# Five transposes ahead of a late weight chunk, and the next tile's transposes one matmul later

## Chip, cores, metric

One core of a Trainium2 chip. The metric is the device time of one execution in microseconds. The kernel before took 253.84 us (median of three runs, 253.70 to 254.02).

In the profile lines PE is the matmul engine and PEld its row of weight loads; DVE is VectorE, ACT ScalarE, and SP the engine that issues the loads from memory. A line gives start (us), duration (us), engine, line of the kernel, operation, written <- read, shapes and count; in square brackets stands how long the engine was idle just before, and what the profile says ended it.

## The reference, cut to what matters

```python
xn = layernorm(x)                        # x: 2048 tokens x 640, bf16
q, k, v = split(xn @ wqkv)               # 640 -> 3 * 640
out = x + local_attention(q, k, v) @ wo + ((xn @ w_gate) * (xn @ w_up)) @ w_down
```

The change concerns the first 18 us only: the layer norm of the first four tiles of 128 tokens, their transposes, and the first Q and K products.

## The kernel before

A recording layer takes operations in program order, finds their dependences and writes one instruction stream for each engine, in that order. The order in which the Python calls stand is the order on PE.

Loads, all issued by SP one after the other. The Q weights come in five chunks (c, 128 input channels each), then K's:

```python
x_load(1)
for c in range(NCH): wqkv_load(0, c)     # Q weights, chunks 0..4
x_load(2); x_load(3)
for c in range(NCH): wqkv_load(1, c)     # K weights
for t in range(4, 8): x_load(t)
x_load2(8); wqkv_load(2)                 # ... V weights in one piece
```

A tile is normalised by DVE into XNS, transposed by PE in five pieces into PSUM and copied to XNT. For tile 1 DVE copies pieces 0 and 1, ScalarE pieces 2 to 4 (some lines cut):

```python
def tr(t, c0=0):
    ln_pe(t, c0)        # transposes c0..4 of tile t on PE
    ln_copy(t)          # the copies PSUM -> XNT
    if t == 1: ...      # layer norm of tiles 2 and 3 on DVE

def proj_tile(which, t, b, bm, at={}):   # Q (which = 0) of one tile, 25 matmuls of 128 columns
    for c, m in [(c, m) for c in range(NCH) for m in range(NCH)]:
        if (c, m) in at: at[c, m]()
        ... matmul of weights chunk c, column block m, with XNT[:, c, tile t]

bm = 1
proj_tile(0, 0, 0, bm, {(4, 0): lambda: ln_pe(1, 0, 2), (4, 3): lambda: tr(1, 2)})
part_evac(0, 0, 1, 0, 4, 0, 0)
proj_tile(0, 1, 2, bm)
...
for c in range(NCH):                     # K of tiles 0 and 1, 25 matmuls of 256 columns
    if c in (2, 3): tr(c)
    for m in range(NCH): ...
```

After this come Q and K of tiles 2 and 3 (50 matmuls of 256 columns), then V (512 columns) and everything else, without a pause in the matmul stream.

Of the kernel before, what the change touches and what calls it, by code (L numbers as in the profile page):

```python
# [215 lines left out]
def build_kernel(nc, A_x, A_wqkv, A_wo, B_x, B_w_gate, B_w_up, B_w_down, out):  # L216
# [145 lines left out]
    def tp_view(t, c0, c1):  # L362
        b = tp_banks[t % 2]
        if t == 0:
            b = (6, 3, 3, 4, 4)[c0]
        if t == 1 and c0 > 1:
            b = 4
        if t == 2 and c0 > 2:
            b = 5
        return PS[:, b, :].bitcast(BF16)[:, c0 * 128:c1 * 128].rearrange("p (c f) -> p c f", c=c1 - c0)  # L370

    def ln_stats_a(t):
        if t >= NT:
            return
        x, st = XST[:, t % NXS, :], STATS[:, t % 2, 0:12]
        op("dve", lambda e: e.bn_stats(st[:, 0:6], x[:, 0:DHALF]), r=[x[:, 0:DHALF]], w=[st], name=f"bna{t}")

    def ln_stats_b(t):
        if t >= NT:
            return  # L380
        x, st = XST[:, t % NXS, :], STATS[:, t % 2, 0:12]
        op("dve", lambda e: e.bn_stats(st[:, 6:12], x[:, DHALF:D]), r=[x[:, DHALF:D]], w=[("stb", t)], name=f"bnb{t}")

    def ln_aggr(t):
        if t >= NT:
            return
        st, mv, sd = STATS[:, t % 2, 0:12], MV[:, t, 0:2], SD[:, t, 0:1]
        op("dve", lambda e: e.bn_aggr(mv, st), r=[st, ("stb", t)], w=[mv], name=f"bnag{t}")
        op("act", lambda e: e.activation(sd, mv[:, 1:2], ACT.Sqrt, bias=EPSC[:, 0:1]), r=[mv, EPSC[:]], w=[("sd", t)],
           name=f"sd{t}")  # L390
# [13 lines left out]
    def ln_rstd(t):  # L404
        if t >= NT:
            return
        sd, rstd = SD[:, t, 0:1], SD[:, t, 1:2]
        op("dve", lambda e: e.reciprocal(rstd, sd), r=[("sd", t)], w=[("rstd", t)], name=f"rstd{t}")

    def ln_apply(t, between=None):  # L410
        if t >= NT:
            return
        x, xs, mv = XST[:, t % NXS, :], XNS[:, t % NXN, :], MV[:, t, 0:2]
        sd, rstd = SD[:, t, 0:1], SD[:, t, 1:2]
        op0 = ALU.add if t == 1 else ALU.subtract
        mean = ("nm", t) if t == 1 else mv
        if between is None:
            ln_rstd(t)
        else:
            between()  # L420
        for c0, c1 in {0: ((0, 128), (128, D)), 1: ((0, 256), (256, D))}.get(t, ((0, D),)):
            o, i = xs[:, c0:c1], x[:, c0:c1]
            op("dve", (lambda o, i: lambda e: e.tensor_scalar(o, i, mv[:, 0:1], rstd, op0=op0, op1=ALU.mult))(o, i),
               r=[i, mean, ("rstd", t)], w=[o], name=f"lnap{t}")
        if t >= NTP:
            o = XNT[:, :, t * TS:(t + 1) * TS]
            op("sp", lambda e: e.dma_start_transpose(o, xs), r=[xs], w=[o], dma=True, name=f"xT{t}")
        if t == 7:
            x_load(13)
            x_load2(14)  # L430
        if t == NT - 1:
            late_loads()

    def ln_pe(t, c0=0, c1=NCH):
        for c in range(c0, c1):
            o = tp_view(t, c, c + 1)[:, 0, :]
            i = XNS[:, t % NXN, c * 128:(c + 1) * 128]
            op("pe", (lambda o, i: lambda e: e.transpose(o, i, IDENT[:]))(o, i), r=[i, IDENT[:]], w=[o], name=f"tr{t}_{c}")  # L438

    def ln_copy(t, only=(0, 1, 2)):  # L440
        parts = ((("dve", 0, 1), ("dve", 1, 3), ("dve", 3, NCH)), (("dve", 0, 2), ("act", 2, NCH)),
                 (("dve", 0, 3), ("act", 3, NCH)), (("act", 0, NCH),))[t]
        for k, (eng, c0, c1) in enumerate(parts):
            if k not in only:
                continue
            o = XNT[:, c0:c1, t * TS:(t + 1) * TS]
            tpv = tp_view(t, c0, c1)
            if eng == "dve":
                op("dve", (lambda o, i: lambda e: e.tensor_copy(o, i))(o, tpv), r=[tpv], w=[o], name=f"xntcp{t}_{c0}")
            else:  # L450
                op("act", (lambda o, i: lambda e: e.activation(o, i, ACT.Copy))(o, tpv), r=[tpv], w=[o],
                   name=f"xntcp{t}_{c0}")
# [15 lines left out]
    def wcols(which, c, m):  # L468
        return WQKV[:, which, c, m:D:NCH]
# [19 lines left out]
    def proj_tile(which, t, b, bm, at={}):  # L489
        for c, m in [(c, m) for c in range(NCH) for m in range(NCH)]:  # L490
            if (c, m) in at:
                at[c, m]()
            o = PS[:, b, m * TS:(m + 1) * TS] if m < 4 else PS[:, bm, t * TS:(t + 1) * TS]
            l, x = wcols(which, c, m), XNT[:, c, t * TS:(t + 1) * TS]
            st, sp = c == 0 and m in (0, 4), c == NCH - 1 and m in (3, 4)
            op("pe", (lambda o, l, x, st, sp: lambda e: e.matmul(o, l, x, start=st, stop=sp))(o, l, x, st, sp),  # L496
               r=[l, x], w=[o], name=f"pp{which}_{m}_{t}_{c}")
# [8 lines left out]
    def part_evac(which, t0, nt, m0, nm, b, col):  # L506
        p = 0 if which == 0 else PAD
        o = (QH, KH)[which][0][:, m0:m0 + nm, p + t0 * TS:p + (t0 + nt) * TS]
        i = PS[:, b, col:col + nm * nt * TS].rearrange("p (m s) -> p m s", m=nm)
        sc = SCALE if which == 0 else 1.0  # L510
        op("act", lambda e: e.activation(o, i, ACT.Copy, scale=sc), r=[PS[:, b, :]], w=[o], name=f"ppev{which}_{m0}_{t0}")
# [224 lines left out]
    def ln_start(t):  # L736
        ln_stats_a(t)
        ln_stats_b(t)
        ln_aggr(t)

    def tr(t, c0=0):
        ln_pe(t, c0)
        ln_copy(t)
        if t == 1:
            ln_start(2)
            ln_stats_a(3)
            ln_stats_b(3)
            ln_rstd(2)
            ln_apply(2, lambda: ln_aggr(3))
# [12 lines left out]
            t_ln[0] += 1.45  # L762

    bm = 1
    proj_tile(0, 0, 0, bm, {(4, 0): lambda: ln_pe(1, 0, 2), (4, 3): lambda: tr(1, 2)})
    part_evac(0, 0, 1, 0, 4, 0, 0)
    proj_tile(0, 1, 2, bm)
    part_evac(0, 1, 1, 0, 4, 2, 0)
    ln_apply(3)
    for c in range(NCH):  # L770
        if c in (2, 3):
            tr(c)
        for m in range(NCH):
            o = PS[:, bm, 2 * TS:] if m == 4 else PS[:, 3 + m // 2, m % 2 * 2 * TS:(m % 2 + 1) * 2 * TS]
            l, x = wcols(1, c, m), XNT[:, c, 0:2 * TS]
            st, sp = c == 0 and m % 2 == 0, c == NCH - 1 and m in (1, 3, 4)
            op("pe", (lambda o, l, x, st, sp: lambda e: e.matmul(o, l, x, start=st, stop=sp))(o, l, x, st, sp),  # L777
               r=[l, x], w=[o], name=f"pw1_{m}_0_{c}")
# [9 lines left out]
    for g in range(5):  # L788
# [6 lines left out]
        else:  # L795
            which, m = ((0, 0), (0, 2), None, (1, 0), (1, 2))[g]
# [161 lines left out]
def bass_parallel_sum__sliding_local_dilated__glu_gated_bilinear__prompt_kernel(  # L958
    nc, A_x, A_wqkv, A_wo, B_x, B_w_gate, B_w_up, B_w_down, out
):  # L960
    build_kernel(nc, A_x, A_wqkv, A_wo, B_x, B_w_gate, B_w_up, B_w_down, out)
# [28 lines left out]
```

## Time and profile before

| | kernel before |
|---|---|
| time, median of 3 | 253.84 us |
| span of the profiled execution | 251.6 us |
| PE busy | 248.1 us (99%) |
| first load of K's weights into the array | 9.26 us |
| first matmul of Q, K for tiles 2 and 3 | 12.60 us |
| first of the last five matmuls | 248.89 us |

PE is the bound. Weight loads run ahead of their matmuls (9.26 against 9.31 us for K's first), so the start of a load shows best when PE was let go. I therefore follow one landmark through all runs, the first load of K's weights. The profile lines themselves stand in the prediction.

### The profile page before, as it was taken

The page shows a single profiled execution, that of the slowest core. Times are in us where ns is not written, and L with a number is a line of the kernel's source. Part 1 is how long each engine was busy: PE and PEld are TensorE (multiplying, and loading weights), DVE is VectorE, ACT ScalarE, POOL GpSimd, SP SyncE. Part 2 cuts the span into 40 slices and gives each one's busy share as a digit, 9 for nine tenths or more (in the row PEclk, how much of TensorE's full clock was granted, in tenths as well). Part 3 has the DMA queues.
Part 4 walks back from the last instruction along what each step waited for, and adds up shares of the span by engine and source line. Part 5 has one row for each costly group of instructions (what it writes and reads, how often), then busy time and mean ns, then how long its engine had stood idle before and what let it go on. Part 6 is the DMA issues. An engine that isn't in the chain of part 4 may idle for free.

```text
span 251.6 us, 3277 instructions
## 1 busy us (share of the span) xinstructions
PE 248.1 (99%) x1294; PEld 128.7 (51%) x1294; DVE 215.7 (86%) x255; ACT 114.6 (46%) x203; POOL 32.5 (13%) x41
## 2 busy tenths in 40 slices
PE   8999999999999999999999999999999999999996
PEld 3995555555544444444444444444444444445775
DVE  4898799999999953999999994999999999995221
ACT  5486657555555557555555553225555011111000
POOL 1000001044434231002331110002000000200200
DMA  6999779774777462355369942297500011581651
GB/s 187 311 261 209 110 200 411 170 122 86 129 146 135 76 125 42 140 197 104 63 126 268 453 151 42 42 337 57 89 0 3 21 42 21 76 114 23 95 136 52
DMA packets 33775, 33.78 MB, mean 134 GB/s; under 512 B 17984, under 2 KB 30272, under 8 KB 33728
## 3 DMA queue, kind: packets, MB, share of 16 engines
q1 hardware_dynamic: 27280, 24.13, 33.8%
q0 software_dynamic: 6192, 9.31, 22.8%
q8 instruction: 10, 0.16, 0.3%
q10 hardware_dynamic: 288, 0.13, 0.2%
q14 instruction: 5, 0.04, 0.1%
HBM read 14.42 MB, written 4.59 MB: 76 GB/s over the span
## 4 chain that ended last, share of the span: by engine, by line
PE 96%; DMA 1%; SPq 1%; issue 0%; DVE 0%
PE PS L642 41%; PE PS L669 22%; PE PS L479 21%; PE PS L701 7%; PE PS L503 2%; DMA WQKV<-in_A_wqkv_dram 1%; PE PS L777 1%; SPq L298 1%; PE PS L496 1%; PE PS L438 0%; DVE FOUT L705 0%
## 5 line engine op out<-in xcount | busy, mean ns | idle before, releaser
L642 PE MATMUL PS<-XNT,WU 128*128 128x512 bf16 x240 | 59.6, 379 | 0.0
L642 PE MATMUL PS<-XNT,WG 128*128 128x512 bf16 x240 | 59.6, 379 | 0.0
L479 PE MATMUL PS<-XNT,WQKV 128*128 128x512 bf16 x250 | 54.1, 379 | 0.0
L609 DVE TENSOR_TENSOR PVB<-VO,ATB 128x10240 f16<-128x10240 bf16 x8 | 43.9, 5490 | 0.2
L479 PEld LDWEIGHTS PS<-XNT,WQKV 128*128 128x128 bf16 x250 | 29.4, 118 | 24.4
L644 ACT ACTIVATE USX<-PS 128x512 bf16<-128x512 f32 x48 | 28.7, 597 | 22.6 <-PE PS L642 22.2
L642 PEld LDWEIGHTS PS<-XNT,WU 128*128 128x128 bf16 x240 | 23.5, 98 | 28.3
L642 PEld LDWEIGHTS PS<-XNT,WG 128*128 128x128 bf16 x240 | 23.5, 98 | 28.3
L604 DVE TENSOR_TENSOR PVB<-PVB 128x5120 f16<-128x5120 f16 (+1 forms) x16 | 34.5, 2156 | 0.3
L537 POOL DMA_DIRECT2D LOG<-PE x24 | 21.9, 924 | 58.4 <-DMA LOG<-PE 58.4
L644 ACT ACTIVATE HT<-PS 128x512 bf16<-128x512 f32 x36 | 21.5, 597 | 16.4 <-PE PS L642 16.4
L675 ACT ACTIVATE DT<-PS 128x512 f16<-128x512 f32 x15 | 8.9, 596 | 42.7 <-PE PS L669 42.7
L669 PE MATMUL PS<-HT,WD 128*128 128x512 bf16 x120 | 27.5, 379 | 0.0
L526 DVE TENSOR_TENSOR TMP<-QH,KH 128x2048 f16<-128x2048 bf16 x16 | 19.2, 1219 | 0.0
L669 PEld LDWEIGHTS PS<-HT,WD 128*128 128x128 bf16 x120 | 11.7, 98 | 14.2
L526 DVE TENSOR_TENSOR PP<-QH,KH 128x2048 f16<-128x2048 bf16 x16 | 18.9, 1219 | 0.0
L669 PE MATMUL PS<-VO,WO 128*128 128x512 bf16 x75 | 18.6, 379 | 0.0
L531 DVE TENSOR_TENSOR PP<-PP,TMP 128x4096 f16<-128x4096 f16 x8 | 18.3, 2291 | 0.2
L705 DVE TENSOR_TENSOR FOUT<-PS,XR 128x320 bf16<-128x320 f32 (+2 forms) x9 | 4.1, 455 | 15.4 <-PE PS L701 15.4
L537 POOL DMA_DIRECT2D PE<-PP x8 | 8.3, 1043 | 63.0 <-DVE PP L532 63.0
L647 DVE TENSOR_TENSOR HT<-HT,USX 128x512 bf16<-128x512 bf16 x36 | 14.4, 418 | 1.7 <-ACT USX L644 1.7
L486 ACT ACTIVATE VO<-PS 128x512 bf16<-128x512 f32 x20 | 11.9, 596 | 8.5 <-PE PS L479 8.4
(71 smaller groups left out, 221.4 us busy)
## 6 DMA issues: line engine op xcount, KB each, us to landing
PE<-PP POOLq DMA_DIRECT2D x8, 512.0 KB, 4.8
ATB<-LOG SPq DMA_DIRECT2D x8, 512.0 KB, 4.9
LOG<-PE POOLq DMA_DIRECT2D x24, 128.0 KB, 2.7
WG<-in_B_w_gate_dram SPq DMA_DIRECT2D x1, 1920.0 KB, 7.9
WU<-in_B_w_up_dram SPq DMA_DIRECT2D x1, 1920.0 KB, 14.6
WD<-in_B_w_down_dram SPq DMA_DIRECT2D x1, 1920.0 KB, 10.1
out_dram<-in_A_x_dram SPq DMA_DIRECT2D x1, 1920.0 KB, 10.3
out_dram<-FACC POOLq DMA_DIRECT2D x3, 640.0 KB, 6.7
```

What stands on the lines that cost most here:

```text
L479: op("pe", (lambda l, x, c: lambda e: e.matmul(PS[:, b, :], l, x, start=(c == 0), stop=(c == NCH - 1)))(l, x, c), r=[l, x], w=[PS[:, b, :] ...
L486: op("act", lambda e: e.activation(o, PS[:, b, :], ACT.Copy, scale=sc), r=[PS[:, b, :]], w=[o], name=f"pev{which}_{m}_{j}")
L526: return (1.22, lambda: op("dve", lambda e: e.tensor_tensor(o, qw, kw, ALU.mult), r=[q, k], w=[o], name=f"prod{h}_{p}_{c}"))
L531: (2.3, lambda: op("dve", lambda e: e.tensor_tensor(a, a, b, ALU.add), r=[a, b], w=[a], name=f"psum{h}_{p}")),
L537: op("pool", lambda e: e.dma_start(o, i, accum_op=ALU.add), r=[o, i], w=[o], dma=True, name=name)
L604: return lambda: op("dve", lambda e: e.tensor_tensor(o, x, y, ALU.add), r=[x, y], w=[o], name=f"{name}_{b}")
L609: lambda: op("dve", lambda e: e.tensor_tensor(PVB[:], vw, aw, ALU.mult), r=[v, a], w=[PVB[:]], name=f"pv_{b}")),
L642: op("pe", (lambda l, x, c: lambda e: e.matmul(PS[:, b, :], l, x, start=(c == 0), stop=(c == NCH - 1)))(l, x, c), r=[l, x], w=[PS[:, b, :] ...
L644: op("act", lambda e: e.activation(o, PS[:, b, :], ACT.Copy), r=[PS[:, b, :]], w=[o], name=f"guev{which}_{m}_{j}")
L647: h_pending.append(lambda: op("dve", lambda e: e.tensor_tensor(h, h, o, ALU.mult), r=[h, o], w=[h], name=f"h{m}_{j}"))
L669: op("pe", (lambda l, x, i: lambda e: e.matmul(PS[:, b, :], l, x, start=(i == 0), stop=(i == n - 1)))(l, x, i), r=[l, x], w=[PS[:, b, :]], ...
L701: op("pe", (lambda l, x, i, b, wid: lambda e: e.matmul(PS[:, b, 0:wid], l, x, start=(i == 0), stop=(i == n - 1)))(l, x, i, b, wid), r=[l, ...
```

## The change

The intent is to use the time in which PE waits for the last chunk of the Q weights. All of tile 1's transposes, two of which stood ahead of that chunk and three behind its third matmul, now stand ahead of it. As PE should then reach tile 2's transposes sooner, these go behind one more matmul.

```diff
-    proj_tile(0, 0, 0, bm, {(4, 0): lambda: ln_pe(1, 0, 2), (4, 3): lambda: tr(1, 2)})
+    proj_tile(0, 0, 0, bm, {(4, 0): lambda: tr(1)})
...
     for c in range(NCH):
-        if c in (2, 3):
-            tr(c)
         for m in range(NCH):
+            if (c, m) in ((2, 1), (3, 0)):
+                tr(c)
```

Only PE's order changes; DVE, ScalarE, GpSimd and SP have the same instructions in the same order.

## The prediction

> **What bounds the kernel now.** I read the page first, then the chain of waits, then the stretch from 5 to 19 us instruction by instruction, because the change touches nothing else. The page says who is full:
>
> ```profile
> PE 248.1 (99%) x1294; PEld 128.7 (51%) x1294; DVE 215.7 (86%) x255; ACT 114.6 (46%) x203; POOL 32.5 (13%) x41
> ```
>
> A matmul engine that is busy 99% of the span can gain only in its few holes or by dropping instructions, and the change drops none. The chain that ended last shows where the unbroken matmul stream begins:
>
> ```profile
> 3.55 3.73 DMA WQKV<-in_A_wqkv_dram
> 7.28 0.05 issue
> 7.33 0.36 PE PS L496 x3
> ...
> 249.34 0.02 issue
> ```
>
> The fifth chunk (c = 4) of the Q weights is issued at 3.55 and lands at 7.28 us; from the matmul it releases at 7.33 the chain is PE alone until the last evacuation. The list of waits gives PE one more hole only, 1.0 us at the very start. So a microsecond saved just behind 7.33 us is a microsecond off the end, unless a later input is not ready. The timeline of that stretch (start, duration, engine, line, operation):
>
> ```profile
> 6.73 0.37 DVE L423 TENSOR_SCALAR XNS<-XST,MV,SD 128x384 bf16<-128x384 bf16 x1
> 6.87 0.28 PE L438 MATMUL PS<-IDENT,XNS 128*128 128x128 bf16 x2
> 7.32 0.21 PEld L496 LDWEIGHTS PS<-XNT,WQKV 128*128 128x128 bf16 x3 [0.34 <-DMA WQKV<-in_A_wqkv_dram]
> 7.33 0.36 PE L496 MATMUL PS<-XNT,WQKV 128*128 128x128 bf16 x3 [0.17 <-DMA WQKV<-in_A_wqkv_dram]
> 7.53 0.33 PE L438 MATMUL PS<-IDENT,XNS 128*128 128x128 bf16 x3
> 7.70 1.78 PE L496 MATMUL PS<-XNT,WQKV 128*128 128x128 bf16 x27
> 7.89 0.49 ACT L451 ACTIVATE XNT<-PS 128x384 bf16<-128x384 bf16 x1 [1.66 <-PE PS L438]
> 9.31 1.26 PE L777 MATMUL PS<-XNT,WQKV 128*128 128x256 bf16 x10
> 9.78 0.39 DVE L423 TENSOR_SCALAR XNS<-XST,MV,SD 128x640 bf16<-128x640 bf16 x1
> 10.29 0.37 PEld L438 LDWEIGHTS PS<-IDENT,XNS 128*128 128x128 bf16 x5
> 10.40 0.44 PE L438 MATMUL PS<-IDENT,XNS 128*128 128x128 bf16 x5
> 10.43 0.45 DVE L423 TENSOR_SCALAR XNS<-XST,MV,SD 128x640 bf16<-128x640 bf16 x1
> ```
>
> Two things are to be seen. First, the weight-load row stands still for 0.34 us before 7.32: two transposes of tile 1 are done, the third to fifth are queued behind matmuls that need the late chunk, although their input is complete at 6.73 + 0.37 = 7.10. Second, there is a hole that the waits do not name. From 7.70 to 9.31 are 27 matmuls in 1.61 us, which is 60 ns each, while the 128-column matmuls near the end of the kernel start every 56 ns (12 from 248.22 to 248.89). 27 x 0.0558 = 1.506, so 0.10 us is missing. Narrow windows find it in the weight loads:
>
> ```profile
> 8.26 0.12 PEld L496 LDWEIGHTS PS<-XNT,WQKV 128*128 128x128 bf16 x1
> ```
>
> ```profile
> 8.44 0.12 PEld L496 LDWEIGHTS PS<-XNT,WQKV 128*128 128x128 bf16 x1
> ```
>
> The load due at 8.26 + 0.056 = 8.32 comes at 8.44. It is the first of chunk 2 of tile 1's Q product (two matmuls end tile 0, ten are chunks 0 and 1), which needs the ScalarE copy of transposes 2 to 4. That copy ran from 7.89 to 8.38 and started when the fifth transpose was done. So the late transposes cost PE twice.
>
> **What the Trainium skill says.** "TensorE: Matmul & The Clock Gate", section "Wait — 56ns, not 53.3ns?": warm matmuls start N / 2.4 GHz + about 2.5 ns apart, 55.6 ns at N = 128. The trace agrees (0.67 us / 12 = 56 ns), and at 256 columns too (50 matmuls from 12.60 to 18.06, 109 ns each). Its section "Part 4: PE-mode transpose" says that a transpose is a matmul into PSUM that needs a copy after it, and gives about 275 ns for one in a kernel's context. Here one is recorded at 220 ns, and in a row they take (7.70 - 7.53) / 3 = 57 ns of the stream; this is what I use. "Perfetto Trace Analysis", section "Tensor Engine Instruction (MATMUL, LD_WEIGHTS)": the recorded end of a matmul is estimated, not observed. Hence I take gaps from starts; the 0.17 us of idle PE that the profile prints beside 0.34 us on the load row is an instance. "DMA: Bandwidth & Descriptors", section "Anatomy of one DMA — SWDGE (gpsimd) path": the DMA engines themselves wait on no semaphore, the issuing sequencer does. SP's order is the same in both kernels, and its weight issues before 10 us stand back to back (0.43 us each), so the landings should stay where they are.
>
> **The change part by part.** Compared engine by engine, only PE's order differs; all counts are equal.
>
> (a) Transposes 2 to 4 of tile 1 move ahead of chunk 4. Earliest start: input ready 7.10, plus the 0.055 us that I see from a DVE end to a PE start (tile 0: 5.11 to 5.16), gives 7.155; loads at 7.155, 7.21 and 7.27, so the fourth slot is 7.32. The chunk's first load was at 7.32. They fit into the hole with nothing left over. Saving: 3 x 0.057 = 0.17 us. Their PSUM target, bank 4, was last read by tile 0's copies, over by 5.97.
>
> (b) The fifth transpose ends about 0.3 us sooner (7.53 + 0.33 = 7.86 before; now start 7.33 + 0.22 = 7.55), so the ScalarE copy runs from about 7.58 to 8.07. Chunk 2 of tile 1 now comes at about 7.33 + 0.03 (restart) + 15 x 0.056 = 8.20. The hidden stall goes: 0.10 us. Chunks 0 and 1 come at 7.64 and need the DVE copy that ended at 7.48 before.
>
> Sum offered to the K product: 0.17 + 0.10 = 0.27 us.
>
> (c) What can take it back. The first K chunk was needed by a load at 9.26. The issue queue and the landing view:
>
> ```profile
> 4.97 2.33 SPq L298 DMA_DIRECT2D WQKV<-in_A_wqkv_dram  x5
> ```
>
> ```profile
> WQKV<-in_A_wqkv_dram SPq DMA_DIRECT2D x1, 160.0 KB, 4.0
> ```
>
> So K chunk 0 lands at 4.97 + 4.0 = 8.97 (the 4.0 is rounded, 8.92 to 9.02), and with the 0.04 us from landing to load seen at 7.28 and 7.32 the load can start at 9.01. Room: 0.25 us. Chunk 1: load 9.80, ready 5.44 + 4.0 + 0.04 = 9.48, room 0.32. Chunk 2 now meets its first matmul where the transposes of tile 2 stood, 10.29: issued 5.91, 4.1 to landing, ready 10.05, room 0.24.
>
> (d) Tile 2's transposes one matmul later. XNS of tile 2 is ready at 9.78 + 0.39 + 0.055 = 10.225, fixed by DVE, which waited for x of tile 2 at 7.74 and for nothing on PE since. Shifted by 0.25 the transposes would come in the load row at 10.04 and wait 0.18. The matmul put ahead takes 0.11 of that, and since loads run 0.11 us ahead of their matmuls (10.29 against 10.40), the rest costs PE at most a few hundredths. Tile 3's transposes: ready 10.43 + 0.45 + 0.055 = 10.935, matmul at 11.23 - 0.25 = 10.98: just in time. Tile 3's ScalarE copy moves with them, its engine free from about 11.43.
>
> (e) Behind that: V's weights land at 9.71 + 7.8 = 17.51, needed by a load at 17.95 (room 0.40); token tiles 4 to 7 land by 18.74 + 4.2 = 22.94, needed near 23.4 (room about 0.4). The attention output for the first down projection is done at 149.95 and used at 152.31. No cap below 0.27.
>
> The smallest room is 0.24 to 0.25, and a stall restarts with a loss of some 0.03. I put the gain at 0.22 us: 253.84 - 0.22 = 253.62 us, or 0.09%.
>
> **The rivals.** *The wait only moves.* If K chunk 0 lands at 9.02 or later in most runs, or tile 2's input is the true gate, 0.05 to 0.15 us comes back: 253.70 to 253.80. For it: the room in (c) and (d) equals the gain almost exactly, and the transfer queue has no slack. Against: four separate gates all leave about 0.24, and the author's matmul ahead of tile 2's transposes opens the tightest. *Transposes get in the way.* If tile 1's second normalisation ends later than 7.10 in other runs, or the wait on it costs more, the three transposes delay chunk 4 by 0.05 to 0.15 us and gain little: 253.75 to 253.95. For it: they fit with nothing left over. Against: even if late, they only go back to where they were, and (b) stays. *The gain is hidden later*, by DVE or a transfer: 253.84. Against: PE waits nowhere after 7.33, with 2.36 us of room at the first down projection. A gain above 0.3 us has no source.
>
> **Range and chances.** The three runs before spread over 0.32 us (253.70 to 254.02), more than the whole effect, so the range is mostly that noise around 253.62: 253.30 to 253.95. Two per cent is 5.1 us, twenty times what the holes hold: within 2% 0.985; faster 0.005; slower 0.01, for an unforeseen state of the chip.
>
> **What would show it.** Right: five transposes in a row from about 6.87, the fifth starting near 7.33; the load of chunk 4 still near 7.32; the ScalarE copy of tile 1 near 7.58 instead of 7.89; 30 matmuls without a hole; the first 256-wide matmul near 9.05 instead of 9.31; the first 512-wide one near 17.84 instead of 18.06. Wrong: chunk 4's load after 7.40 with a wait on DVE; a wait for the weights at K's chunk 0 or 2, or for XNS before tile 2's transposes, longer than 0.1 us; or a first 512-wide matmul 0.2 us earlier with an unchanged end, which would mean that something past 18 us holds the end.

## The result

| | before | after |
|---|---|---|
| median of 6 runs | 253.58 us | 253.34 us |
| all runs | 253.22 to 254.02 | 253.17 to 253.74 |
| span of the profile | 251.6 us | 251.6 us |
| first of the last five matmuls | 248.89 us | 248.82 us |

The ratio is 0.9992 with a 95% interval of 0.9979 to 1.0005. Ratios here are not quite the ratio of the medians. The time lies inside the range and in the class that was predicted, and the ratio of 0.9992 is 0.2 us, near the 0.22 us forecast; but the interval contains 1, which is no effect, and the profile shows only 0.07 us at the end (248.89 - 248.82). The hit on the time is luck in part. The median of the kernel before over all six runs, 253.58, lies in the predicted range as well, so no effect at all would have met it; and the forecast point, 253.62, was worked out from the first three runs (253.84), which were the slower ones. The timeline of the changed kernel at the same place:

```profile
6.76 0.32 PEld L496 LDWEIGHTS PS<-XNT,WQKV 128*128 128x128 bf16 x5 [0.32 <-DVE SD L408]
6.79 0.45 PE L496 MATMUL PS<-XNT,WQKV 128*128 128x128 bf16 x5 [0.20 <-DMA WQKV<-in_A_wqkv_dram]
7.02 0.32 PEld L438 LDWEIGHTS PS<-IDENT,XNS 128*128 128x128 bf16 x5
7.30 1.87 PEld L496 LDWEIGHTS PS<-XNT,WQKV 128*128 128x128 bf16 x30
7.38 0.29 DVE L449 COPY XNT<-PS 128x256 bf16<-128x256 bf16 x1 [0.27 <-PE PS L438]
7.55 0.49 ACT L451 ACTIVATE XNT<-PS 128x384 bf16<-128x384 bf16 x1 [1.30 <-PE PS L438]
9.21 1.14 PEld L777 LDWEIGHTS PS<-XNT,WQKV 128*128 128x128 bf16 x11
```

Several steps look as forecast. The five transposes stand in a row, the load of chunk 4 comes at 7.30 (forecast 7.32), and the ScalarE copy starts at 7.55 (forecast 7.58). Yet the 30 loads last from 7.30 to 9.17. At 0.056 us each the last would end at 7.30 + 29 x 0.0557 + 0.12 = 9.04, so the matmuls are not "without a hole". The first transpose came at 7.02 instead of 6.87, because chunk 3 of the Q weights, on time in the profile before, was late: PE waited for it ahead of 6.79. And K's first load at 9.21 is later than the stream offers: the last load before it begins at 9.05, so 9.11 was due. That remainder is K's own weight chunk 0, issued at 4.97 and 4.2 us on its way:

```profile
WQKV<-in_A_wqkv_dram SPq DMA_DIRECT2D x1, 160.0 KB, 4.2
```

4.97 + 4.2 = 9.17. In the profile before it was 4.0. Two more signs that the prediction named came out short: K's first matmul started at 9.21 (forecast 9.05, before 9.31), and V's first at 17.99 (forecast 17.84, before 18.06; its record is missing, so 17.99 is the second one's 18.21 less 0.216 for one matmul).

A scan of the weight loads in narrow windows finds the hole between two neighbouring loads of the changed kernel:

```profile
7.52 0.12 PEld L496 LDWEIGHTS PS<-XNT,WQKV 128*128 128x128 bf16 x1
...
7.73 0.12 PEld L496 LDWEIGHTS PS<-XNT,WQKV 128*128 128x128 bf16 x1
```

It stands in front of tile 1's chunk 0 (five loads after 7.30), which needs DVE's copy of the first two transposes: 7.38 + 0.29 = 7.67. So the ScalarE copy, part (b) of the prediction, no longer holds anything up, and the other copy does in its place.

**Theories.** From here on two theories stand against each other. *As predicted:* the change saves up to 0.27 us, minus what later landings take. *New:* K's start is set by a chain from tile 1's first two transposes through DVE's copy to tile 1's first chunk, and what PE does meanwhile is hidden, in either order; the hole ahead of chunk 4, from which the prediction took its 0.17 us, is an accident of one execution. A third possibility is that nothing has an effect and 0.2 us is chance.

### The profile page after: what moved, and what is told of

It is laid out like the page before. It is cut to its first block, busy times and chain, and to the rows that moved or that the text cites. A ratio compares the mean times of both kernels' runs of the same rounds, so it can differ in the third digit from the quotient of the medians.

```text
span 251.6 us, 3257 instructions
## 1 busy us (share of the span) xinstructions
PE 246.9 (98%) x1274; PEld 128.9 (51%) x1294; DVE 215.9 (86%) x255; ACT 114.6 (46%) x203; POOL 32.6 (13%) x41
## 3 DMA queue, kind: packets, MB, share of 16 engines
q0 software_dynamic: 6192, 9.31, 22.7%
## 4 chain that ended last, share of the span: by engine, by line
PE 91%; DVE 3%; SPq 2%; DMA 2%; issue 1%; ACT 0%
PE PS L642 41%; PE PS L669 22%; PE PS L479 21%; PE PS L701 7%; SPq L298 2%; DMA XST<-in_A_x_dram 2%; DVE STATS L376 1%; DVE STATS L382 1%; DVE MV L388 0%; DVE XNS L423 0%; ACT SD L389 0%; DVE FOUT L705 0%; DVE SD L408 0%
## 5 line engine op out<-in xcount | busy, mean ns | idle before, releaser
L642 PE MATMUL PS<-XNT,WU 128*128 128x512 bf16 x237 | 59.0, 379 | 0.2
L642 PE MATMUL PS<-XNT,WG 128*128 128x512 bf16 x232 | 57.9, 379 | 0.4
```

The lines of the kernel that those rows point to most:

```text
L642: op("pe", (lambda l, x, c: lambda e: e.matmul(PS[:, b, :], l, x, start=(c == 0), stop=(c == NCH - 1)))(l, x, c), r=[l, x], w=[PS[:, b, :] ...
```

## The experiments

Every kernel ran five rounds (one set has six runs of it). Those of one group ran on one chip and share the runs of the kernel before: group 1 median 253.56 us, group 2 253.58, group 3 253.71. All results are correct, except two.

### Group 1: both kernels again, and each half of the change

**before_again** is the kernel before, no edit.

> The kernel before, unchanged, against itself: the noise floor, and a second profile of it. My theory: ratio 1.000 with an interval of about 0.1% either way; in its profile the hidden stall ahead of chunk 2 of tile 1's Q product is there again (27 matmuls in about 1.61 us instead of 1.51), and the first 256-wide matmul starts at 9.3 whatever the landing of K's first chunk, as long as that is before 9.2. Rival (the 0.24 us between the medians is chance): the two sets of this kernel differ by 0.2 us as well.

Ratio 0.9998 (0.9985 to 1.0010), as expected. But the profile shows another execution than the first one. The weight loads:

```profile
6.92 0.32 PEld L496 LDWEIGHTS PS<-XNT,WQKV 128*128 128x128 bf16 x5 [0.56 <-DVE XNS L423]
7.18 0.15 PEld L438 LDWEIGHTS PS<-IDENT,XNS 128*128 128x128 bf16 x2
7.34 0.21 PEld L496 LDWEIGHTS PS<-XNT,WQKV 128*128 128x128 bf16 x3
9.27 1.05 PEld L777 LDWEIGHTS PS<-XNT,WQKV 128*128 128x128 bf16 x10
```

PE stood still before chunk 3 (6.92; the profile names DVE beside the load and the weights' DMA beside the matmul, and 3.07 + 3.7 = 6.77 for the landing fits the DMA). Behind the two transposes there is almost no hole left: 7.24 + 0.056 would be 7.30, and chunk 4 loads at 7.34. The 27 matmuls do take 1.61 us again, with 0.10 us missing, as I expected. They miss it at another place:

```profile
7.71 0.12 PEld L496 LDWEIGHTS PS<-XNT,WQKV 128*128 128x128 bf16 x1
...
7.89 0.12 PEld L496 LDWEIGHTS PS<-XNT,WQKV 128*128 128x128 bf16 x1
```

7.89 is the first load of tile 1's chunk 0, and DVE's copy ran from 7.55 to 7.84. So "the hidden stall ahead of chunk 2 again" was a miss: the same loss has a different cause.

**after_again** is the changed kernel, no edit.

> The changed kernel again. My theory: what the matmul stream gains is the smaller of 0.27 us and what the landing of K's first chunk leaves. If that chunk lands at 8.97 again, as in the profile of the kernel before, the first 256-wide matmul starts near 9.05 and the last five matmuls near 248.70; if at 9.17, as in the first profile of this kernel, at 9.21 and 248.82. Ratio 0.9990 to 0.9997. Rival (no effect at all, the landing eats everything): first 256-wide matmul at 9.3 and ratio 1.000.

Ratio 0.9991 (0.9977 to 1.0004). The profile:

```profile
7.08 0.32 PEld L438 LDWEIGHTS PS<-IDENT,XNS 128*128 128x128 bf16 x5
7.36 1.87 PEld L496 LDWEIGHTS PS<-XNT,WQKV 128*128 128x128 bf16 x30
9.16 1.05 PEld L777 LDWEIGHTS PS<-XNT,WQKV 128*128 128x128 bf16 x10
10.57 0.12 PEld L777 LDWEIGHTS PS<-XNT,WQKV 128*128 128x128 bf16 x1 [0.36 <-DMA WQKV<-in_A_wqkv_dram]
```

K's chunk 0 was there early (4.97 + 3.6 = 8.57), and still K's first load came only at 9.16, with the first matmul at 9.22, not near 9.05. Tile 1's chunk 0 loads at 7.79, and again DVE's copy (7.44 + 0.29 = 7.73) lets it go. The last line is a second finding: the late piece was now K's chunk 2, 4.6 us on its way, and it cost as much as the change can give: the next stage started 3.59 us after K's first matmul, where it is 3.29 without a wait. The last five matmuls begin at 249.09.

**tile1_only** leaves tile 2's transposes where they were.

```diff
-            if (c, m) in ((2, 1), (3, 0)):
+            if (c, m) in ((2, 0), (3, 0)):
```

> All five transposes of tile 1 ahead of chunk 4, tile 2's transposes left where they were. My theory: K's first matmul at 9.05 to 9.21 as in the changed kernel, but the transposes of tile 2 come before XNS of tile 2 is there (10.225) unless K's first chunk landed late: they wait up to 0.15 us, and the first matmul of the next stage starts at 12.50 to 12.60 against 12.53 in the changed kernel. Ratio 0.9995 to 1.000. Rival (the second edit is decoration): no wait on XNS of tile 2, same start as the changed kernel.

Ratio 1.0000 (0.9987 to 1.0013). K's first load is at 9.25 and the next stage starts at 12.59. PE came no earlier than in the kernel before, so tile 2's transposes (load at 10.29) did not have to wait, and the run cannot judge the second edit. Its end was lost elsewhere: V's weights took 8.7 us, and V's first product waited for them.

```profile
18.83 1.46 PE L479 MATMUL PS<-XNT,WQKV 128*128 128x512 bf16 x6 [0.61 <-DMA WQKV<-in_A_wqkv_dram]
```

**tile2_only** has the kernel before's order for tile 1 and the new place for tile 2.

> Only tile 2's transposes one matmul later; tile 1 as before. My theory: nothing to gain, since PE does not come early: the first 256-wide matmul at 9.31, the next stage at 12.60, the last five matmuls at 248.89, ratio 1.000. Rival (the second edit carries the gain): next stage 0.1 us or more sooner.

Ratio 0.9990 (0.9977 to 1.0002), the "best" of the group, from an edit that can gain nothing by either theory. Its profile shows no gain: K's chunk 2 was late here too (0.35 us of waiting in the load row), and the last five matmuls begin at 249.04. This ratio is a measure of chance: a difference of 0.1% is not evidence in five rounds.

### Group 2: the copies and the landings

**one_behind** puts transposes 2 to 4 behind the first matmul of chunk 4.

```diff
-    proj_tile(0, 0, 0, bm, {(4, 0): lambda: ln_pe(1, 0, 2), (4, 3): lambda: tr(1, 2)})
+    proj_tile(0, 0, 0, bm, {(4, 0): lambda: ln_pe(1, 0, 2), (4, 1): lambda: tr(1, 2)})
```

> The kernel before with transposes 2 to 4 of tile 1 behind the first matmul of chunk 4 instead of the third. Part (a) of my sum is absent (they still stand behind the late chunk), part (b) is there: the ScalarE copy starts 0.11 us sooner, near 7.78, and the hidden stall of 0.10 us goes. Theory: first 256-wide matmul at 9.20 to 9.22 if K's first chunk allows, 27 + 3 matmuls and 3 transposes without a hole. Rival (the 0.10 us is not the copy but something of the matmuls themselves, as a PSUM bank turn): the gap stays in front of chunk 2 and the start stays 9.31.

Ratio 0.9997 (0.9984 to 1.0009). The ScalarE copy started earlier, at 7.69. K's first load came at 9.40, behind its own weights (4.97 + 4.4 = 9.37). The 29 loads ahead of it start at 7.43 and end at 9.14, where 7.43 + 28 x 0.0557 + 0.12 = 9.11 would be without a stall: 0.03 us are missing instead of 0.10. But the stall did not go, it moved: transposes 2 to 4 had to wait for their own input (ready at 6.88 + 0.37 = 7.25, first load at 7.30), and tile 1's chunk 0 still loads at 7.70, 0.69 us after the first transpose at 7.01. Without its late chunk K was due at 9.14 - 0.12 + 0.056 = 9.08, 2.07 us after the first transpose; in the other runs without a hole it is 2.08 to 2.09. Where in this stretch PE loses its time makes no difference: the first half of what the new theory says.

**seven_later** puts transposes 2 to 4 and their copy into tile 1's own product, seven matmuls later.

```diff
-    proj_tile(0, 0, 0, bm, {(4, 0): lambda: ln_pe(1, 0, 2), (4, 3): lambda: tr(1, 2)})
-    part_evac(0, 0, 1, 0, 4, 0, 0)
-    proj_tile(0, 1, 2, bm)
+    proj_tile(0, 0, 0, bm, {(4, 0): lambda: (ln_pe(1, 0, 2), ln_copy(1, (0,)))})
+    proj_tile(0, 1, 2, bm, {(1, 0): lambda: (tr(1, 2), part_evac(0, 0, 1, 0, 4, 0, 0))})
```

(In `tr`, tile 1 then copies only pieces 2 to 4.)

> The kernel before with transposes 2 to 4 of tile 1 seven matmuls later (in chunk 1 of tile 1's product), its copy with them. Theory: the ScalarE copy starts 7 x 0.056 = 0.39 us later, near 8.28, ends near 8.77, and the stall ahead of chunk 2 grows from 0.10 to about 0.5 us; first 256-wide matmul near 9.70, next stage near 12.99, last five matmuls near 249.28, ratio 1.0015 (0.39 / 253.6). Rival (later gates swallow it, as they would a gain): next stage at 12.7 or earlier, ratio 1.000.

Ratio 1.0015 (1.0002 to 1.0027), as expected, the only kernel of the first two groups that is clear of chance. The profile loses more, 249.58 - 248.89 = 0.69 us, because there are two stalls:

```profile
7.90 0.32 PEld L496 LDWEIGHTS PS<-XNT,WQKV 128*128 128x128 bf16 x5 [0.26 <-DVE XNT L449]
8.58 0.49 ACT L451 ACTIVATE XNT<-PS 128x384 bf16<-128x384 bf16 x1 [2.23 <-PE PS L438]
9.12 0.88 PEld L496 LDWEIGHTS PS<-XNT,WQKV 128*128 128x128 bf16 x15 [0.46 <-ACT XNT L451]
```

The second is the one expected (ScalarE's copy, about 0.5). The first is DVE's copy before tile 1's chunk 0, and here it is large enough for the profile to name it. The first transpose was at 7.19 and chunk 0 at 7.90: 0.71 us. In before_again it is 7.89 - 7.18 = 0.71, in the changed kernel 7.73 - 7.02 = 0.71, in after_again 7.79 - 7.08 = 0.71. That is the chain of the new theory. PE has ten loads to issue in that time in the order of either kernel (two transposes, three transposes, five matmuls), 10 x 0.056 = 0.56 us, and 0.15 us stay empty. With transposes 2 to 4 gone from it, more stays empty.

**no_landing** is the changed kernel with Q's weights in K's first three chunks. Its output is wrong, which doesn't matter for the time.

```diff
-            l, x = wcols(1, c, m), XNT[:, c, 0:2 * TS]
+            l, x = wcols(1 if c > 2 else 0, c, m), XNT[:, c, 0:2 * TS]
```

> The changed kernel, but K's first three chunks multiply with Q's weights, which are in SBUF long before: a wrong result on purpose, to take the landings of K's chunks 0 to 2 out of the way. Theory: first 256-wide matmul at about 9.03 (7.35 + 30 x 0.056), then the transposes of tile 2 stand against XNS (about 10.23) and the next stage starts at 12.36 to 12.42; last five matmuls at 248.65 to 248.72, time 0.1 us below the changed kernel. Rival (the gate at K's start is not the landing but the change of shape or the switch of PSUM banks): first 256-wide matmul still near 9.2.

Ratio 0.9991 (0.9978 to 1.0005). There was no wait at K, although its chunk 0 landed at about 4.97 + 4.4 = 9.37. But K's first load came at 9.29, because the chain began at 7.20: chunk 3 of Q was late again (load at 6.94). 7.20 + 0.71 + 25 x 0.0557 = 9.30. So the 9.03 that I expected was a miss; I had still reckoned from chunk 4.

**no_landing_before** is the same edit in the kernel before.

> The same wrong weights in the kernel before: a control. Theory: nothing changes, as the landing did not bind there: first 256-wide matmul at 9.31, next stage at 12.60, ratio 1.000. Rival (the landing already cost the kernel before some tenths in most runs): faster by 0.1 us or more.

Ratio 0.9999 (0.9986 to 1.0011). The profile contradicts my number: K's first load came at 9.00, the earliest of all standard load orders, in the *old* order, since its first transpose was at 6.92 (6.92 + 2.10 = 9.02). It also shows what the second edit is for. Tile 2's transposes, which stand where they did before, now had to wait, as their input was there at 9.74 + 0.39 = 10.13:

```profile
10.19 0.45 PE L438 MATMUL PS<-IDENT,XNS 128*128 128x128 bf16 x5
```

The matmul was due at 9.05 + 10 x 0.109 = 10.14, so the loss is 0.05 us, the "few hundredths" of the prediction. And it shows how little an early K stage is worth: the next stage started at 12.39 instead of 12.60, then V's first product waited 0.59 us for its weights (8.7 us on their way), and the last five matmuls began at 249.44, later than in any other run of that load order but seven_later (249.58) and level with tile1_only.

### Group 3: the hole made on purpose, and a better place

**hole_before** and **hole_after** are the two kernels with two loads exchanged, so that chunk 4 of Q is always late.

```diff
-    for c in range(NCH):
+    for c in range(NCH - 1):
         wqkv_load(0, c)
     x_load(2)
+    wqkv_load(0, NCH - 1)
```

> The kernel before with two loads exchanged: x of tile 2 ahead of chunk 4 of the Q weights, so that this chunk lands late in every run, near 7.72 us (4.02 + 3.7), well behind the first transposes of tile 1. What I now hold: the first profile of the kernel before was such a case by chance (hole of 0.34 us before chunk 4) and eight later ones were not. In the case, the order of before costs 1.94 us from the load of chunk 4 to the first load of K, as it did there (7.32 to 9.26). Expected: chunk 4 at 7.6 to 7.85, K 1.94 later if its own weights have landed. Rival (the chain from the first transposes of tile 1 decides alone): K 2.09 after the first transpose, whatever chunk 4 does.

> The changed kernel with the same exchanged loads. If the change works as predicted once the hole is there, the five transposes and the copies finish inside it and K's first load comes 30 x 0.0557 + 0.03 = 1.70 us after the load of chunk 4, 0.24 us less than the 1.94 of the kernel before under the same loads; the end comes 0.24 us sooner unless the weights of V hold it. Rival (the order never matters): 1.94 here too.

hole_before took 254.22 us, ratio 1.0020 (1.0005 to 1.0034); hole_after 253.70 us, ratio 1.0000 (0.9988 to 1.0012). Weight loads of hole_before, then of hole_after (line numbers are one higher here):

```profile
7.60 0.15 PEld L439 LDWEIGHTS PS<-IDENT,XNS 128*128 128x128 bf16 x2
8.16 0.21 PEld L497 LDWEIGHTS PS<-XNT,WQKV 128*128 128x128 bf16 x3 [0.41 <-DMA WQKV<-in_A_wqkv_dram]
10.10 1.05 PEld L778 LDWEIGHTS PS<-XNT,WQKV 128*128 128x128 bf16 x10
```

```profile
7.38 0.32 PEld L439 LDWEIGHTS PS<-IDENT,XNS 128*128 128x128 bf16 x5
7.89 1.72 PEld L497 LDWEIGHTS PS<-XNT,WQKV 128*128 128x128 bf16 x30 [0.19 <-DMA WQKV<-in_A_wqkv_dram]
9.55 1.16 PEld L778 LDWEIGHTS PS<-XNT,WQKV 128*128 128x128 bf16 x11
```

From chunk 4 to K: 10.10 - 8.16 = 1.94 us in the old order, exactly as in the first profile of the kernel before, and 9.55 - 7.89 = 1.66 us in the new one, with no stall among the 30. I had expected 1.70 here. The rival that the order never matters (1.94 in both) falls. Where the hole exists, the change saves 0.28 us, the predicted sum of 0.27. This is also where it shows by the clock: the means of the six runs and the five on the same chip are 254.20 and 253.70 us, 0.5 us apart, with a standard error of 0.14 that I estimate from their scatter. What exceeds 0.28 is chance or other landings (chunk 4 itself came 0.27 us sooner in the second profile), which these runs do not separate.

**three_two** starts the chain sooner: the first two transposes stand ahead of chunk 3, which is where PE waits in most profiles.

```diff
-    proj_tile(0, 0, 0, bm, {(4, 0): lambda: tr(1)})
+    proj_tile(0, 0, 0, bm, {(3, 0): lambda: ln_pe(1, 0, 2), (4, 0): lambda: tr(1, 2)})
```

> The changed kernel with the first two transposes of tile 1 one chunk earlier, ahead of chunk 3, the other three still ahead of chunk 4. What I now hold: in most runs the hole is in front of chunk 3, and what sets K's start is the chain first transposes of tile 1, DVE copy, tile 1's first chunk (0.71 us), which in both kernels starts only behind chunk 3. Here it runs in the hole. Expected where chunk 3 lands late (load after 6.8): K's first load 2.15 us after the load of chunk 3, against 2.35 in both kernels (6.92 to 9.27, and 6.76 to 9.11 without its wait), so 0.2 us sooner, unless K's weights hold it; 30 matmuls without a stall. Where chunk 3 is on time: no loss, since the hole is then ahead of chunk 4. Ratio 0.9985 to 0.9995. Rival (the stall before tile 1's chunk 0 is a turn of PSUM banks, not the copy): it stays, and K starts 2.3 us behind chunk 3.

Ratio 0.9992 (0.9980 to 1.0005).

```profile
6.82 0.12 PEld L438 LDWEIGHTS PS<-IDENT,XNS 128*128 128x128 bf16 x2
7.32 0.32 PEld L496 LDWEIGHTS PS<-XNT,WQKV 128*128 128x128 bf16 x5 [0.38 <-DMA WQKV<-in_A_wqkv_dram]
7.58 0.21 PEld L438 LDWEIGHTS PS<-IDENT,XNS 128*128 128x128 bf16 x3
7.75 1.73 PEld L496 LDWEIGHTS PS<-XNT,WQKV 128*128 128x128 bf16 x30
9.42 1.16 PEld L777 LDWEIGHTS PS<-XNT,WQKV 128*128 128x128 bf16 x11
```

From chunk 3 to K it is 9.42 - 7.32 = 2.10 us, with 30 loads in 1.67 us and no stall. With chunk 3 late, both other kernels need 2.35 (before_again 6.92 to 9.27, tile1_only 6.90 to 9.25, no_landing 6.94 to 9.29). Of the 0.25 us between them, 2 x 0.056 = 0.11 us are the two transposes themselves, which now fill the wait ahead of chunk 3. The rest is the stall: the other kernels have 40 loads in this stretch, 40 x 0.0557 = 2.23 us, so 0.12 us of their 2.35 are empty; here it is 38 loads, 2.12 us, and nothing is empty. The chain of the new theory is confirmed by taking it away. The rival (a turn of PSUM banks) falls, as it would have kept the stall. But in this execution chunk 3 was 4.2 us on its way instead of the 3.2 to 3.8 of the other runs in this load order, and the gain was gone: the last five matmuls begin at 249.05.

**three_two_v** also loads V's weights ahead of x of tiles 8 and 9.

```diff
-    x_load2(8)
     wqkv_load(2)
+    x_load2(8)
```

> The kernel three_two with V's weights loaded ahead of x of tiles 8 and 9. Three of ten profiles so far had V's first product wait for its weights (landing near 18.4 instead of 17.5). Expected: they are issued 0.5 us sooner with 320 KB less in front of them, and land near 16.5 to 17.5; no wait on them at V's first product, the end where three_two has it or 0.1 us sooner on average. Rival (x of tiles 8 and 9 now come too late and DVE or the transposing DMA holds up the second group of Q and K): a wait of PE after 23 us.

Ratio 0.9993 (0.9980 to 1.0006). V's weights were 7.4 us on their way from their earlier issue near 9.2, so landed near 16.7, and nothing waited for them, nor did PE wait anywhere after 19 us. The first load of K is at 9.02, of chunk 3 at 6.90 (2.12 us), the next stage starts at 12.36, and the last five matmuls begin at 248.66, the earliest of all 14 profiles. By the clock it is not shown to beat the changed kernel: 253.53 us against 253.71 of the kernel before in the same rounds.

### The profiles of both orders in one table

First weight load of tile 1's first transpose, of Q's chunk 4 and of K, in us.

| run | order of tile 1 | transpose | chunk 4 | K | transpose to K |
|---|---|---|---|---|---|
| before | old | 6.87 | 7.32 | 9.26 | 2.39 |
| before_again | old | 7.18 | 7.34 | 9.27 | 2.09 |
| tile2_only | old | 7.03 | 7.16 | 9.12 | 2.09 |
| no_landing_before | old | 6.92 | 7.07 | 9.00 | 2.08 |
| after | new | 7.02 | 7.30 | 9.21 (9.11 without K's late chunk) | 2.19 (2.09) |
| after_again | new | 7.08 | 7.36 | 9.16 | 2.08 |
| tile1_only | new | 7.16 | 7.44 | 9.25 | 2.09 |
| no_landing | new | 7.20 | 7.48 | 9.29 | 2.09 |
| hole_before | old | 7.60 | 8.16 | 10.10 | 2.50 |
| hole_after | new | 7.38 | 7.89 | 9.55 | 2.17 |

Without a hole ahead of chunk 4 both orders need 2.08 to 2.09 us, which is 0.71 for the chain and 25 x 0.0557 = 1.39 for tile 1's product. With a hole the old order needs 2.39 and 2.50. Of the four profiles of the old order under standard loads, one has the hole: the one that the prediction was made from. The landings say why. In it chunk 4 of Q landed 1.02 us after chunk 3 (6.26 and 7.28), in the other eleven profiles with this order of Q's loads 0.43 to 0.58 us after it. PE has seven loads to issue between the two (five of chunk 3, two transposes), 7 x 0.056 = 0.39 us, which covers most of that.

## Why the prediction was right, and where it was wrong

**PE as the bound, a class of "within 2%", the range.** Right. No kernel here left 253 to 255 us.

**(a) Three transposes in the hole, 0.17 us, and (b) the ScalarE copy, 0.10 us.** Right for the execution that was profiled, and shown by the pair with exchanged loads: 1.94 against 1.66 us, a saving of 0.28 for a forecast of 0.27. As a forecast for an ordinary execution the sum was too large. The failing term is the assumption under it, "the landings should stay where they are". They do not: chunk 3 of Q was 3.2 us on its way in the first profile and 3.5 to 4.2 in the other thirteen. This load, issued at 3.07, in the first profile and in before_again:

```profile
WQKV<-in_A_wqkv_dram SPq DMA_DIRECT2D x1, 160.0 KB, 3.2
```

```profile
WQKV<-in_A_wqkv_dram SPq DMA_DIRECT2D x1, 160.0 KB, 3.7
```

With chunk 3 late the transposes start later and chunk 4 is there by the time they are done. There is no hole to fill, and three transposes more ahead of chunk 4 only push it back (7.36 to 7.48 in three profiles of the new order).

**"Chunks 0 and 1 come at 7.64 and need the DVE copy that ended at 7.48 before".** This step failed, as it rests on the same assumption. It took the time of the copy from an execution in which the first transposes ran at 6.87. The copy moves with them, and chunk 0 cannot follow the first transpose by less than 0.71 us. Where a hole ahead of chunk 4 covers that time the step holds (hole_after: no stall among the 30 loads). Where there is none, this stall stands in both orders, and against the first profile one wait is exchanged for another of nearly the same length: 0.12 us ahead of chunk 2 (8.32 to 8.44) there, 0.15 us ahead of chunk 0 here. So the rival "the wait only moves" was the right one, though with a gate that the prediction had not listed.

**(c) K's first chunk leaves 0.25 us of room.** Right as a gate, wrong as a number: the chunk was 3.6 to 4.4 us on its way, so its room is anything from nothing to more than the gain. In the first profile of the changed kernel it took back 0.10 us. (The load of chunk 1 that the prediction puts at 9.80 was at 9.75, so its room was 0.27 and not 0.32.)

**(d) Tile 2's transposes one matmul later.** Its reason holds: in no_landing_before, where PE came early and the transposes stood in the old place, they cost 0.05 us. In three_two_v, in the new place, the next stage started 12.36 - 9.08 = 3.28 us after K's first matmul, without a loss.

**(e) V's weights leave 0.40 us.** Wrong. They were 7.3 to 8.7 us on their way, and in two of eleven profiles with the standard load order V's first product waited about 0.6 us for them, far more than the change can give; in a third, no_landing, it came 0.12 us late.

**What stays open.** The timed gain, 0.9992 and 0.9991 in two sets on different runs, would fit 0.2 us. Both intervals contain 1, tile2_only reached 0.9990 without a mechanism, and the profiles give nothing in the ordinary case and 0.28 us in the case with a hole. How often the hole occurs in unprofiled executions is not known. Nor is it shown whether it belongs to one execution or to one chip: the profile with the hole is of an execution of 253.41 us, none of the three that were timed, and its chip is not on record, while the groups ran on chips 8, 5 and 15. Why a load's time on its way varies was not looked into. A gain of a few hundredths up to 0.2 us on average is compatible with everything; the runs do not decide it.

## What to carry to other kernels

Work moved into a wait gains only in the executions in which the wait is there; when a load sets it, take several profiles before spending its length, above all when loads queue behind one another. Before moving producers around, follow the chain from each producer through its copy to its first user: work that sits in the shadow of such a latency can be reordered for ever without effect, while starting the chain one step sooner takes the stall away (0.12 us here, in the profile; the clock does not resolve it). The lists of waits here left out stalls of 0.10 to 0.15 us; count instructions against their known spacing instead.

## What the Trainium skill lacked or had wrong

- "TensorE: Matmul & The Clock Gate", "Part 4: PE-mode transpose", says that a copy must follow and gives about 275 ns for a transpose in a kernel. Here one is recorded at 220 ns and takes 56 ns of the stream. What mattered is not on the page: from the first of two transposes through DVE's copy to the load that may use it were 0.69 to 0.71 us in all nine profiles in which nothing else held that load up.
- "DMA: Bandwidth & Descriptors", "Anatomy of one DMA — SWDGE (gpsimd) path", gives about 2.0 us plus bytes over 436 GB/s for one DMA on the GpSimd path, an estimate of 2.4 us for 160 KB. The queued 160 KB chunks of weights, issued by SP and so not on that path, took 2.4 to 4.6 us here. How much one and the same load varies between executions I found as a figure on no page: 3.2 to 4.2 us for Q's chunk 3, 3.6 to 4.4 for K's chunk 0, 7.3 to 8.7 for V's 800 KB.
